# One attention-and-SwiGLU kernel on one core: the opening by sets, the short last set as one quarter, and DMAs in other slots of the schedule

## The chip, the core and the metric

The kernel runs on one core of a Trainium2 chip. The core has TensorE (PE, matmuls and weight loads), VectorE (DVE), ScalarE (ACT), GpSimd (POOL) and SyncE (SP), which here only issues DMAs. Each engine executes its own instructions in order and waits on semaphores for the others. The metric is device time in microseconds (us) of one execution, the median of several.

## The reference

Four batches (B) of N = 12416 tokens with C = 128 channels go through an induced set attention with m = 32 inducing points, and the result through a normalized SwiGLU feed-forward of 1536 hidden channels. Cut to what matters:

```python
def mab(q, kv):
    s = scale * (q @ kv.transpose(0, 2, 1))
    s = s - s.max(-1, keepdims=True)
    a = np.exp(s)
    a /= a.sum(-1, keepdims=True) + 1e-09
    return a @ kv
h = mab(I, x)                 # 32 rows per batch
attn = mab(x, h)              # 12416 rows per batch
# then, for every token:
rms = np.sqrt(np.mean(x * x, axis=-1, keepdims=True) + 1e-06)
xn = x / rms * rms_g
g = xn @ w_gate
silu = g * (1.0 / (1.0 + np.exp(-g)))
val = xn @ w_val
out = silu * val @ w_out
```

The three weight matrices arrive as 64-bit floats and have to be rounded to 32 bits on the chip; `x` and the inducing points are 32-bit.

## The kernel before

**Tiling.** The 97 blocks of 128 tokens of a batch are cut into seven sets: five of 16 blocks, one of 15 and a short last one of 2 (`per`). A set is four quarters of 32 partitions each. The attended row of a token is a combination of the 32 rows of `h`, so the normalized input of the feed-forward is 32 weights per token (`a`, scaled by `rs`) times `h`; the gate and value matrices are therefore folded with `h` into two stacks of 32 rows per batch (`sg`, `sv`). Both the weights and the stacks are split in a high and a low half (`hi`, `lo`), and four combinations of halves, 4 x 32 = 128 rows, make one matmul. A **unit** is one quarter of a set, up to 512 tokens; the short set is one unit of 256 tokens, for which its four quarters are put side by side. So a batch has 25 units.

**The feed-forward** (`ffn`) runs one unit in 12 **steps**, one for each 128 hidden channels: a gate matmul (L460), a value matmul (L462), silu on ACT (L464), a product `u` on DVE (L466), and two steps later the output matmul into `acc` (L448; 32-bit, in two passes). After the last step DVE transposes `acc` into `o` (L451) and four DMAs store it (L455); for the short set sixteen do.

**What a unit needs.** `gather` (L434) brings the quarter's `hi` and `lo` rows four times under each other into a moving tile `a`: four DMAs on SP, sixteen for the short set. It is issued at step 2 of the unit before. `hi` and `lo` come from the steps of `seam`: `turn_a`, `square`, `scale`, `apply` and `split`. `split` transposes the weights (L419), casts them into `hi` (L421) and writes the rest into `lo` (L422). The pool `halves` has one buffer, so `split` of a set waits until the gather of the last unit of the set before has landed. In the table `seams`, `split` stands at step 4 of the third unit of the set before.

**Two batches at once.** While the 300 steps of a batch run, `schedule` puts the attention of the next batch between them, each piece at a step number `k` from 0 to 299: transposes of x, `scores1`, the maxima, one exponential over the whole batch (`exp1`), `turn_e` and `sum_h` by set, `end_h`, `turn_h`, `square_h`, the fetches of the gate and value weights (`fetch`, L352), `stack`, and the second scores and softmax. `sum_h` also issues the loads of the rows of x of the batch after the next one (`load_rows`, L115), as soon as the set's tile is used. `stack` multiplies the weights with `h` (L361), rounds and splits them, and issues the 12 DMAs that place them in the stack (L371). All these DMAs go through SP in the order in which the code issues them; at most eight are under way.

**The opening.** The first batch has no feed-forward to hide behind. Its x is loaded by rows, transposed on PE (L248) and copied by ACT (L251); `scores1`, the maxima, `exp1` and `sum_h` follow. Between these pieces `convert` puts the rounding of nine weight chunks of 128 x 512: six DVE passes and three POOL passes for each (L204 to L216), cut into six steps. A chunk's buffer is free for the next raw chunk when its result has been stored (L188). Then follow `stack` for both matrices, the first set's `seam`, the first gather, and unit 0.

The order on every engine is thus written by hand: by the order of the calls in the opening, and by the step numbers of `schedule` and `seams` after it.

Of the kernel before, what the change touches and what calls it, by code (L numbers as in the profile page):

```python
# [18 lines left out]
P = 128  # L19
R = 4  # L20
# [4 lines left out]
def kernel(  # L25
# [32 lines left out]

    nc = tc.nc
# [10 lines left out]
    assert N % P == 0 and full >= 2 and rest < 12  # L70
    per = [16] * full if not rest else [16] * (full - 1) + [15, rest + 1]
    NS = len(per)
    start = [P * sum(per[:s]) for s in range(NS)]
    cols = [slice(m * sum(per[:s]), m * sum(per[:s + 1])) for s in range(NS)]
    SCW = N // R

    units = [(s, q, 1) for s in range(full) for q in range(R)] + [(s, 0, R) for s in range(full, NS)]
    assert all(per[s] * nq <= 16 for s, _, nq in units)
# [23 lines left out]
    def of(dram, b, s):  # L102

        d = dram[ds(b * N + start[s], P * per[s]), :]
        return d.rearrange("(i q t) c -> q i t c" if b else "(q i t) c -> q i t c", q=R, i=m)
# [4 lines left out]
    def load_rows(b, s):  # L110
        n = per[s]
        t = xnat[b, s] = xnp.tile([P, n, C], F32, name=f"xn{s}")
        if b:
# [63 lines left out]
    def load_w(i, c):  # L177
# [14 lines left out]
        if not wide:  # L192
# [4 lines left out]
        e, s = (up.tile([P, 512], I32, name="u") for _ in range(2))  # L197
        f = astk.tile([P, 512], F32, name="a")
        r = outp.tile([P, 512], F32, name="o")
        fi = f.bitcast(I32)  # L200
        ve = nc.vector
        ge = ve if (i, c) == (1, NC - 1) else nc.gpsimd
        return [
            lambda: ve.tensor_scalar(out=e[:], in0=high, scalar1=20, scalar2=0x7FF,  # L204
                                     op0=ALU.logical_shift_right, op1=ALU.bitwise_and),
            lambda: ve.tensor_scalar(out=e[:], in0=e[:], scalar1=896.0, scalar2=1151.0, op0=ALU.max, op1=ALU.min),
            lambda: ve.tensor_scalar(out=s[:], in0=high, scalar1=-(1 << 31), scalar2=0x3F800000,
                                     op0=ALU.bitwise_and, op1=ALU.bitwise_or),
            lambda: (ve.tensor_scalar(out=fi[:], in0=high, scalar1=12, scalar2=9,
                                      op0=ALU.logical_shift_left, op1=ALU.logical_shift_right),  # L210
                     ge.tensor_scalar(out=e[:], in0=e[:], scalar1=-896.0, scalar2=float(1 << 23), op0=ALU.add, op1=ALU.mult)),
            lambda: ve.scalar_tensor_tensor(out=r[:], in0=low.bitcast(U32), scalar=2.0 ** -52, in1=s.bitcast(F32)[:],
                                            op0=ALU.mult, op1=ALU.mult),
            lambda: (ve.tensor_tensor(out=fi[:], in0=fi[:], in1=s[:], op=ALU.bitwise_or),
                     ge.tensor_tensor(out=f[:], in0=f[:], in1=r[:], op=ALU.add),
                     ge.tensor_tensor(out=dst, in0=f[:], in1=e.bitcast(F32)[:], op=ALU.mult),  # L216
                     put()),
        ]
# [3 lines left out]
    def attention(b, load_next):  # L222
# [12 lines left out]
        def turn_x(s, k):  # L235
# [9 lines left out]
            if now:  # L245
# [5 lines left out]
                nc.scalar.copy(out=dst, in_=src)  # L251

        def scores(s, lhsT):
            w = per[s] * m
            ps = bank()
            for q in range(R):
                nc.tensor.matmul(ps[ts(q, m), 0:w], lhsT, xT[b, s][:, ts(q, w)], start=True, stop=True)  # L257
            return ps[:, 0:w]

        def scores1(s):  # L260
            nc.vector.tensor_scalar(out=sc[b][:, cols[s]], in0=scores(s, indT[:]), scalar1=1.0, scalar2=None,
# [21 lines left out]
        def exp1():  # L283
            hl = st["hl"] = once.tile([P, C + 1], F32, name="hl")
            nc.scalar.activation(sc[b][:], sc[b][:], AF.Exp, bias=st["nbias"][:], scale=SCALE, accum_out=hl[:, C:C + 1])  # L285

        def turn_e(s):
            e = st["e", s] = work.tile([P, per[s] * m], F32, name="e", tag="work")
            nc.vector.transpose(out=e[:], in_=sc[b][:, cols[s]])

        def sum_h(s):
# [3 lines left out]
            ps = bank()  # L295
# [7 lines left out]
            if load_next:  # L303
                load_rows(b + 1, s)
# [337 lines left out]
```

## Time and profile before

| what | value |
|---|---|
| median of 3 runs | 1890.85 us (1885.89 to 1890.9) |
| the profiled execution's own time | 1892.92 us |
| its span (first to last instruction) | 1891.1 us |
| mean granted PE clock | 0.962 of full speed |
| PE busy | 1731.8 us, 92% |
| DVE, ACT, POOL busy | 1141.6, 757.4, 176.8 us |
| first matmul of the feed-forward | at 94.1 us |
| last matmul | ends at 1881.2 us |

A row of a wait view reads: the engine and line that waited, what it waited for, the total, how often, and the longest. A row of a timeline reads: start, duration, engine, line, operation, output and inputs, count; in brackets the engine's idle time before it and what ended that. SPq is SP's queue of DMA issues: the time there is that of issuing, not that of the transfer. PE's matmul rows overlap; the distance from start to start tells the pace.

### The profile page before, as it was taken

How to read it: one execution, taken by the hardware profiler on the slowest of the kernel's cores; microseconds unless marked ns; L12 is line 12 of the kernel's file. 1: busy time of each engine (PE TensorE's matmuls, PEld its weight loads, DVE VectorE, ACT ScalarE, POOL GpSimd, SP SyncE). 2: the span in 40 equal slices, each digit the busy share in tenths (PEclk: the TensorE clock that was granted, in tenths of full speed). 3: DMA queues.
4: the chain of work that ended last, by engine and by line, in shares of the span. 5: the costliest groups of instructions: out<-in, count | busy, mean ns of one | idle time of the engine just before them, and what ended most of it. 6: DMA issues, size and time to landing. Idle time of an engine off the chain costs nothing.

```text
span 1891.1 us, 20393 instructions
## 1 busy us (share of the span) xinstructions
PE 1731.8 (92%) x6258; PEld 961.9 (51%) x6258; DVE 1141.6 (60%) x1998; ACT 757.4 (40%) x1256; POOL 176.8 (9%) x141
## 2 busy tenths in 40 slices
PE   6199999989979999998997999998998999999997
PEld 4045555545545555554555555554454655555554
DVE  5567765546546776565654776564655665655654
ACT  3044444323524444532453444532353444444443
POOL 2221110101011011010110110110101101100100
PEclk8599999989989999999998999998998999999998
DMA  7744313533324212434333311122111211111111
GB/s 271 173 77 84 58 32 70 127 76 57 58 45 78 45 25 40 94 95 92 59 57 61 66 37 29 27 48 57 42 33 19 40 30 28 34 34 33 28 36 19
DMA packets 393517, 114.05 MB, mean 60 GB/s; under 512 B 369056, under 2 KB 373184, under 8 KB 390848
## 3 DMA queue, kind: packets, MB, share of 16 engines
q1 hardware_dynamic: 393216, 112.73, 29.0%
q8 instruction: 50, 0.82, 0.2%
q14 instruction: 59, 0.48, 0.1%
q10 hardware_dynamic: 192, 0.02, 0.0%
HBM read 53.95 MB, written 27.00 MB: 43 GB/s over the span
## 4 chain that ended last, share of the span: by engine, by line
PE 82%; DMA 5%; SPq 5%; DVE 3%; ACT 2%; issue 2%; POOL 0%; DVEq 0%; ACTq 0%
PE acc L448 50%; PE gv L460 14%; PE gv L462 13%; SPq L434 3%; DMA xn<-in_x_dram 2%; DMA a<-lo 2%; PE mm L257 2%; DVE u L466 1%; PE mm L398 1%; DMA a<-hi 1%; PE mm L297 1%; ACT silu L464 1%; SPq L455 1%; PE gv L257 0%; ACT sc L285 0%
## 5 line engine op out<-in xcount | busy, mean ns | idle before, releaser
L448 PE MATMUL acc<-u,wo 128*128 128x512 f32 (+2 forms) x2400 | 1220.9, 592 | 58.5 <-DVE u L466 58.2
L466 DVE TENSOR_TENSOR u<-silu,gv 128x512 f32<-128x512 f32 (+2 forms) x1200 | 796.4, 670 | 606.6 <-ACT silu L464 594.0
L464 ACT ACTIVATE silu<-gv 128x512 f32<-128x512 f32 (+2 forms) x1200 | 699.4, 584 | 1046.4 <-PE gv L460 545.3
L460 PE MATMUL gv<-a,sg 128*128 128x512 f32 (+2 forms) x1200 | 932.2, 777 | 60.1 <-DMA a<-lo 57.1
L448 PEld LDWEIGHTS acc<-u,wo 128*128 128x128 f32 x2400 | 444.9, 191 | 216.1 <-DVE u L466 73.4
L462 PE MATMUL gv<-a,sv 128*128 128x512 f32 (+2 forms) x1200 | 471.3, 393 | 0.6 <-DVE u L466 0.6
L460 PEld LDWEIGHTS gv<-a,sg 128*128 128x128 f32 x1200 | 230.9, 192 | 348.9 <-issue 326.3
L462 PEld LDWEIGHTS gv<-a,sv 128*128 128x128 f32 x1200 | 231.1, 193 | 276.4 <-issue 193.0
L401 POOL TENSOR_TENSOR z<-z,sc 128x512 f32<-128x512 f32 (+2 forms) x27 | 30.3, 1124 | 1125.6 <-DVE z L400 1104.8
L409 POOL TENSOR_TENSOR rs<-ms,mhalf 128x16 f32<-128x16 f32 (+2 forms) x28 | 71.9, 2568 | 107.2 <-DVE ms L407 107.2
L451 DVE STREAM_TRANSPOSE o<-acc 128x512 f32<-128x512 f32 (+2 forms) x100 | 69.1, 691 | 3.7 <-PE acc L448 3.4
L341 POOL TENSOR_TENSOR sc<-sc,mx 128x512 f32<-128x512 f32 (+2 forms) x24 | 21.9, 914 | 354.5 <-DVE mx L340 354.5
L421 DVE CAST hi<-aT 128x512 fp32r<-128x512 f32 (+2 forms) x28 | 11.0, 391 | 70.0 <-DMA a<-hi 64.7
L240 DVE STREAM_TRANSPOSE xT<-xT 128x512 f32<-128x512 f32 (+2 forms) x84 | 53.1, 633 | 0.0
L398 PE MATMUL mm<-eT,gram 128*128 128x512 f32 (+2 forms) x56 | 27.2, 568 | 5.6 <-DVE eT L389 5.6
L414 POOL TENSOR_TENSOR sc<-sc,rs 128x512 f32<-128x512 f32 (+2 forms) x27 | 25.1, 928 | 2.1
L422 DVE TENSOR_TENSOR lo<-aT,hi 128x512 fp32r<-128x512 f32 (+2 forms) x28 | 17.4, 621 | 11.2 <-DMA a<-lo 10.7
L464 ACT ACT_TABLE_LOAD x8 | 10.3, 1283 | 26.7 <-PE gv L460 26.6
L297 PE MATMUL mm<-xn,e 128*32 128x128 f32 x582 | 20.7, 276 | 0.0
L400 DVE STREAM_TRANSPOSE z<-mm 128x512 f32<-128x512 f32 (+2 forms) x28 | 17.9, 639 | 3.5 <-PE mm L398 3.5
L257 PE MATMUL mm<-xT,indT 128*32 128x512 f32 (+2 forms) x168 | 20.0, 547 | 0.0
L257 PE MATMUL mm<-xT,hT 128*32 128x512 f32 (+2 forms) x168 | 20.0, 547 | 0.0
(126 smaller groups left out, 421.8 us busy)
## 6 DMA issues: line engine op xcount, KB each, us to landing
out_dram<-o SPq DMA_DIRECT2D x320, 64.0 KB, 2.0
xn<-in_x_dram SPq DMA_DIRECT2D x60, 256.0 KB, 4.9
xT<-in_x_dram SPq DMA_DIRECT2D x60, 256.0 KB, 4.6
a<-hi SPq DMA_DIRECT2D x160, 64.0 KB, 2.0
a<-lo SPq DMA_DIRECT2D x160, 64.0 KB, 2.0
w<-w SPq DMA_DIRECT2D x21, 256.0 KB, 3.1
xn<-in_x_dram SPq DMA_DIRECT2D x5, 1024.0 KB, 11.4
out_dram<-o SPq DMA_DIRECT2D x64, 60.0 KB, 2.0
```

What stands on the lines that cost most here:

```text
L240: nc.vector.transpose(out=t[:, ts(k, n * m)], in_=t[:, ts(k, n * m)])
L257: nc.tensor.matmul(ps[ts(q, m), 0:w], lhsT, xT[b, s][:, ts(q, w)], start=True, stop=True)
L297: nc.tensor.matmul(ps[ts(t % R, m), 0:C], e[:, ts(t, m)], xn[:, t, :], start=t < R, stop=t + R >= n)
L398: nc.tensor.matmul(ps[:, 0:n * m], gram[b][:], st["eT"][:], start=True, stop=True)
L409: nc.gpsimd.tensor_tensor(out=rs[:, 0:n], in0=ms[:, 0:n], in1=mhalf[:, 0:n], op=ALU.pow)
L434: nc.sync.dma_start(out=a[ts(k, m), ts(q, w)].bitcast(F32), in_=half[ts(q0 + q, m), 0:w].bitcast(F32))
L448: nc.tensor.matmul(acc[:, 0:T], wo[:, j, :], t[:, 0:T], start=(j == 0), stop=(j == NJ - 1))
L451: nc.vector.transpose(out=o[:, 0:T], in_=acc[:, 0:T])
L460: nc.tensor.matmul(g[:, 0:T], sg[:, ts(j, P)], a[:, 0:T], start=True, stop=True)
L462: nc.tensor.matmul(v[:, 0:T], sv[:, ts(j, P)], a[:, 0:T], start=True, stop=True)
L464: nc.scalar.activation(sl[:, 0:T], g[:, 0:T], AF.Silu)
L466: nc.vector.tensor_tensor(out=t[:, 0:T], in0=sl[:, 0:T], in1=v[:, 0:T], op=ALU.mult)
```

## The change

**The short set as one quarter.** For the second half of the attention and the feed-forward, the short set is now 32 partitions by 8 blocks instead of 128 by 2 (`quarters`, `per2`, `rows2`, `cols2`). Its softmax, `seam` and exponential work on 32 partitions, its exponential is an instruction of its own (`exp2`), and its unit takes four gathering and four storing DMAs.

**The opening.** One exponential for each set (`exp1_of`) and one PSUM bank for the sums of all sets. A chunk's rounding is now four DVE passes, two POOL passes and two ACT passes, in two parts (`parts`, `join`). Every fourth block of transposed x is copied by DVE instead of ACT. The stacks of the first batch are written by `stack_of`: `hg` holds 128 columns, four copies of 32, so that one matmul for each chunk gives all four row groups; ACT casts all of them and DVE subtracts in the lower half. No DMA places them. The first gather issues its `lo` halves from ACT's queue.

**Slots.** `load_rows` of the next batch moves from `sum_h` (and for batch 1 from the opening) to steps 97, 103, ... of the schedule. The second `fetch` moves from step 178 to 193, the second `stack` from 198 to 203, and the placing DMAs go one row group per step (`place`). `split` moves from step 4 to step 9. A store is issued two steps after its transpose (`soon`).

```diff
-    units = [(s, q, 1) for s in range(full) for q in range(R)] + [(s, 0, R) for s in range(full, NS)]
+    quarters = [R] * full + [1]
+    per2 = per[:full] + [R * per[full]]
+    rows2 = [slice(0, m * nq) for nq in quarters]
+    cols2 = columns(per2)
...
+        def parts():
+            ve.tensor_scalar(out=e[:], in0=high, scalar1=20, scalar2=0x7FF, op0=ALU.logical_shift_right, op1=ALU.bitwise_and)
+            nc.gpsimd.tensor_scalar(out=e[:], in0=e[:], scalar1=896.0, scalar2=1151.0, op0=ALU.max, op1=ALU.min)
+            nc.scalar.activation(e[:], e[:], AF.Copy, bias=-896.0 * (1 << 23), scale=float(1 << 23))
+            ve.tensor_scalar(out=f[:], in0=high, scalar1=0xFFFFF, scalar2=None, op0=ALU.bitwise_and)
+            nc.scalar.activation(f.bitcast(F32)[:], f[:], AF.Copy, bias=1.0, scale=2.0 ** -20)
+
+        def join():
+            ve.scalar_tensor_tensor(out=e[:], in0=high, scalar=-(1 << 31), in1=e[:], op0=ALU.bitwise_and, op1=ALU.bitwise_or)
+            ve.scalar_tensor_tensor(out=f.bitcast(F32)[:], in0=low.bitcast(U32), scalar=2.0 ** -52, in1=f.bitcast(F32)[:],
+                                    op0=ALU.mult, op1=ALU.add)
+            nc.gpsimd.tensor_tensor(out=dst, in0=f.bitcast(F32)[:], in1=e.bitcast(F32)[:], op=ALU.mult)
+            put()
...
-                nc.scalar.copy(out=dst, in_=src)
+                if k == 1:
+                    nc.vector.tensor_copy(out=dst, in_=src)
+                else:
+                    nc.scalar.copy(out=dst, in_=src)
...
+        def exp1_of(s):
+            if not s:
+                st["hl"] = once.tile([P, C + 1], F32, name="hl")
+                st["ls"] = small.tile([P, NS], F32, name="gmx")
+            part = sc[b][:, cols1[s]]
+            nc.scalar.activation(part, part, AF.Exp, bias=st["nbias"][:], scale=SCALE, accum_out=st["ls"][:, s:s + 1])
+            if s + 1 == NS:
+                nc.vector.reduce_sum(out=st["hl"][:, C:C + 1], in_=st["ls"][:], axis=AX.X)
...
-            if load_next:
-                load_rows(b + 1, s)
...
-            for k, half in enumerate((hi, hi, lo, lo)):
-                for c in range(NC):
-                    nc.sync.dma_start(out=stacks[b][i][ts(k, m), ts(c, 512)].bitcast(F32),
-                                      in_=half[ts(c, m), :].bitcast(F32))
+        def place(i, k):
+            half = st["halves", i][k // 2]
+            for c in range(NC):
+                nc.sync.dma_start(out=stacks[b][i][ts(k, m), ts(c, 512)].bitcast(F32), in_=half[ts(c, m), :].bitcast(F32))
+
+        def stack_of(i, c):
+            ps = bank()
+            nc.tensor.matmul(ps[:], st["hg"][:], w0.pop((i, c))[:], start=True, stop=True)
+            w, low = stacks[b][i], slice(P // 2, P)
+            nc.scalar.copy(out=w[:, ts(c, 512)], in_=ps[:])
+            nc.vector.tensor_tensor(out=w[low, ts(c, 512)], in0=ps[low, :], in1=w[low, ts(c, 512)].bitcast(F32),
+                                    op=ALU.subtract)
...
         for k, half in enumerate((hi, lo, hi, lo)):
-            for q in range(nq):
-                nc.sync.dma_start(out=a[ts(k, m), ts(q, w)].bitcast(F32), in_=half[ts(q0 + q, m), 0:w].bitcast(F32))
+            queue = nc.scalar if (b, u) == (0, 0) and k % 2 else nc.sync
+            queue.dma_start(out=a[ts(k, m), 0:w].bitcast(F32), in_=half[ts(q, m), 0:w].bitcast(F32))
...
+                soon(2, lambda: store(o))
...
-    for k in ("max1", "max2", "max3", "exp1"):
+    for k in ("max1", "max2", "max3"):
         f[k]()
-    convert(6)
-    for s in range(NS + 1):
-        if s < NS:
-            f["turn_e"](s)
-        if s:
-            f["sum_h"](s - 1)
+    for s in range(NS):
+        f["exp1_of"](s)
+        if not s:
+            convert()
+        f["turn_e"](s)
+        f["sum_h"](s)
+    convert()
...
+                add(97 + 6 * s, load_rows, b + 1, s)
...
-                add(170 + 8 * i, g["fetch"], i)
-                add(191 + 7 * i, g["stack"], i)
+                add(175 + 18 * i, g["fetch"], i)
+                add(191 + 12 * i, g["stack"], i)
+                for k in range(R):
+                    add(193 + 12 * i + k, g["place"], i, k)
...
-                n, j = ((1, 2), (1, 6), (1, 9), (1, 9), (2, 4))[i] if k else ((2, 1), (2, 4), (2, 7), (2, 7), (3, 0))[i]
+                n, j = ((1, 2), (1, 6), (1, 9), (1, 9), (2, 9))[i] if k else ((2, 1), (2, 4), (2, 7), (2, 7), (3, 0))[i]
```

How the instructions stand on the engines, at three places. First ACT in the opening, from the copies of set 1 on, before up to the one exponential. `xT_...` are the transposed x of a set, `u` and `a` a chunk's exponent and mantissa. Before:

```order
L251 COPY xT_191<-gv 128x4x4x32 x4
L251 COPY xT_230<-gv 128x4x4x32 x4
L251 COPY xT_269<-gv 128x4x4x32 x4
L251 COPY xT_308<-gv 128x4x4x32 x4
L251 COPY xT_347<-gv 128x4x4x32 x3
L251 COPY xT_347<-gv 128x3x4x32
L251 COPY xT_385<-gv 128x2x4x32
L285 ACTIVATE sc,hl<-sc,nbias 128x3104
```

And now:

```order
L259 COPY xT_194<-gv 128x4x4x32 x3
L212 ACTIVATE u<-u 128x512
L214 ACTIVATE a<-a 128x512
L259 COPY xT_233<-gv 128x4x4x32 x3
L212 ACTIVATE u<-u 128x512
L214 ACTIVATE a<-a 128x512
L259 COPY xT_272<-gv 128x4x4x32 x3
L259 COPY xT_308<-gv 128x4x4x32 x3
L212 ACTIVATE u<-u 128x512
L214 ACTIVATE a<-a 128x512
L259 COPY xT_347<-gv 128x4x4x32 x2
```

The copies of three of the sets now have two passes of a chunk ahead of them (a fourth chunk's passes stand behind the last copy).

Second, SP at the end of the opening, up to the first gather. `w_119` and `w_120` are stores of rounded chunks. Before:

```order
L115 DMA xn_586<-in_x_dram 32x1920 x4
L115 DMA xn_595<-in_x_dram 32x256 x4
L188 DMA w_119<-silu 128x512
L371 DMA sg<-whi 32x512 x6
L371 DMA sg<-wlo 32x512 x6
L188 DMA w_120<-silu 128x512
L371 DMA sv<-whi 32x512 x6
L371 DMA sv<-wlo 32x512 x6
L434 DMA a<-hi 32x512
```

And now:

```order
L180 DMA sg<-in_moe_w_out_dram 128x4x256
L196 DMA w_119<-silu 128x512
L196 DMA w_120<-silu 128x512
L462 DMA a<-hi 32x512 x2
L132 DMA xT_686<-in_x_dram 32x64x32 x4
```

The 28 row loads of batch 1 (the last two of seven rows are shown) and the 24 placing DMAs have left this stretch.

Third, SP at the end of the first batch, from the last 480-token gather to the first gather of batch 1. Before:

```order
L455 DMA out_dram<-o 480x1x32 x4
L434 DMA a<-hi 32x64 x4
L434 DMA a<-lo 32x64 x4
L434 DMA a<-hi 32x64 x4
L434 DMA a<-lo 32x64 x4
L124 DMA xT_4025<-in_x_dram 32x64x32
L124 DMA xT_4312<-in_x_dram 32x64x32
L455 DMA out_dram<-o 480x1x32 x4
L434 DMA a<-hi 32x512
```

And now:

```order
L462 DMA a<-hi 32x256
L462 DMA a<-lo 32x256
L462 DMA a<-hi 32x256
L462 DMA a<-lo 32x256
L492 DMA out_dram<-o 480x1x32 x4
L132 DMA xT_3942<-in_x_dram 32x64x32
L132 DMA xT_4217<-in_x_dram 32x64x32
L462 DMA a<-hi 32x512
```

The short unit's gather has four DMAs instead of sixteen, and a store stands behind the gather of its unit instead of ahead of it.

231 lines of the change are left out of this document (115 added, 116 removed).

## The prediction

> **What bounds the kernel now.** I read the page first, then the engines' busy time by stretches, then the waits of TensorE (PE), VectorE (DVE) and the DMA queue (SP), and last the chain of waits and the timelines at the places that these named. From the page and from the view by stretches (span; PE, weight loads, DVE, ACT and POOL busy; granted clock, DMA share, GB/s):
>
> ```profile
> span 1891.1 us, 20393 instructions
> PE 1731.8 (92%) x6258; PEld 961.9 (51%) x6258; DVE 1141.6 (60%) x1998; ACT 757.4 (40%) x1256; POOL 176.8 (9%) x141
> ...
> 100.00:1891.00 1791.00, 1687.88 (x5866) 935.51 (x5865) 1085.74 (x1873) 735.50 (x1222) 149.06 (x110) 0.98 0.27 51
> 0.00:100.00 100.00, 43.88 (x393) 26.42 (x394) 55.90 (x126) 21.87 (x35) 27.70 (x31) 0.72 0.76 218
> ```
>
> After 100 us PE is busy nearly all the time and nothing else is near its limit, so PE is the bound, and what can be won is its idle time (103 us there), its half-rate time, and the opening (56 us idle). Who ends PE's waits from 96 us on, who ends DVE's, and who ends SP's (total us, times, longest):
>
> ```profile
> PE acc L448 <- DVE u L466: 58.2, 22, 9.5
> PE gv L460 <- DMA a<-lo: 30.7, 7, 9.0
> ```
>
> ```profile
> DVE hi L421 <- DMA a<-hi: 64.7, 22, 7.8
> DVE lo L422 <- DMA a<-lo: 10.7, 19, 2.1
> ```
>
> ```profile
> SPq L455 <- DVE o L451: 827.4, 83, 15.9
> SPq L352 <- PE mm L361: 80.4, 3, 29.4
> ```
>
> PE waits 58.2 us for products `u` and 30.7 us for moving tiles `a`. The products are late because DVE itself sits in `split`: its cast into `hi` must not overwrite the single buffer while the gather of the set's last unit still reads it (64.7 us). And the gather is late because SP, one queue in order, stands behind stores whose `o` isn't transposed (827 us, mostly free, but not when a gather is next) and behind weight fetches whose buffers PE frees only later (80.4 us in 3). One such wait in the chain (start, us):
>
> ```profile
> 354.30 0.72 DVE o L451
> ...
> 355.04 0.61 SPq L455
> ...
> 357.70 1.15 SPq L352
> ...
> 360.43 0.59 SPq L434
> ...
> 361.06 2.52 DMA a<-hi
> ...
> 363.71 0.44 DVE hi L421
> ```
>
> Four stores and three fetches go before the gather, and DVE's cast waits for its landing. PE's timeline at that place, and at the longest wait for `a`:
>
> ```profile
> 365.51 2.07 PE L448 MATMUL acc<-u,wo 128*128 128x512 f32 x2 [3.13 <-DVE u L466]
> ...
> 368.24 1.28 PE L448 MATMUL acc<-u,wo 128*128 128x512 f32 x2
> ...
> 369.81 1.02 PE L448 MATMUL acc<-u,wo 128*128 128x512 f32 x2
> ...
> 371.13 1.02 PE L448 MATMUL acc<-u,wo 128*128 128x512 f32 x2
> ```
>
> ```profile
> 400.62 0.77 PE L460 MATMUL gv<-a,sg 128*128 128x512 f32 x1 [9.00 <-DMA a<-lo]
> ...
> 401.62 1.91 PE L448 MATMUL acc<-u,wo 128*128 128x512 f32 x2
> ...
> 404.18 1.91 PE L448 MATMUL acc<-u,wo 128*128 128x512 f32 x2
> ```
>
> A step of the feed-forward takes 371.13 - 369.81 = 1.32 us. After the wait of 3.13 us the next two take 2.73 and 1.57: 1.7 us more. After 9.00 us the two that follow take 2.56 and 2.45, and the start 0.5 more: 2.9 us. So a long wait is paid twice, as idle time and as slow matmuls behind it.
>
> **The change part by part.** The sum is made against the profiled execution, whose own time is 1892.92 for a span of 1891.1; the median shown is 1890.85, so I take span and median as one.
>
> *Split, store and gather: -58.2 us.* `split` moves from step 4 to step 9 of the set's third unit. The gather of the last unit still goes out at step 2, so 7 steps (9.2 us) lie between instead of 2 (2.6 us). The gather takes four issues of 0.63 (below) and a landing of 2.0 to 2.5 us, 5 us in all. The store now goes out two steps after its transpose, which puts it behind the gather. At a batch boundary the price was largest:
>
> ```profile
> 536.22 2.47 SPq L434 DMA_DIRECT2D a<-hi  x4
> ...
> 543.80 2.49 SPq L434 DMA_DIRECT2D a<-lo  x4
> ```
>
> ```profile
> 545.04 0.43 DVE L421 CAST hi<-aT 128x512 fp32r<-128x512 f32 x1 [7.81 <-DMA a<-hi]
> 547.51 0.69 DVE L422 TENSOR_TENSOR lo<-aT,hi 128x512 fp32r<-128x512 f32 x1 [2.04 <-DMA a<-lo]
> ```
>
> Sixteen issues for the short set's unit fill 10 us; as one quarter it needs four. What is late next: the gather of the next set's first unit follows `split` after 5 steps instead of 10, but has 10 steps (13 us) until it is read. I find no wait that keeps its cause, and take all 58.2; the bound below is half of it, if SP stays as late as now.
>
> *Waits for `a`: -30.7 us.* Three are at unit 16 of batches 0 to 2: the second fetch stood on SP from step 178, waiting for matmuls of step 191, with unit 16's gather (issued at 182) behind it. It is now issued at 193, and the 24 placing DMAs go three to a step instead of twelve at once. Then SP carries 3 fetches, 12 placings, 4 gathers and 4 stores in unit 16, 23 issues of about 0.6 = 14 us against 15.8 us: it fits, with 2 us to spare, so I add 1 us for the products that wait for a `work` buffer there. The other four waits are at the short unit, whose twelve fewer gathers and twelve fewer stores take 15 us of issue off SP per batch.
>
> *Half-rate matmuls: -27 us.* From below, six long waits (three at unit 16, three at batch boundaries) times 2.9 = 17; from above, the missing 2% of the clock over 1791 us = 36. I take the middle, since the dozen shorter waits cost up to 1.7 each. [...] The row at 365.51, slow after 3.13 us, says that shorter waits cost too, so I stay with 27.
>
> *The opening: -10 us.* It has gains and a loss. The rows, by engine (SP, PE, ACT, POOL):
>
> ```profile
> 45.79 26.64 SPq L115 DMA_DIRECT2D xn<-in_x_dram  x23
> ...
> 73.98 3.77 SPq L371 DMA_DIRECT2D sg<-whi  x6
> ...
> 92.03 0.58 SPq L434 DMA_DIRECT2D a<-lo  x1
> ```
>
> ```profile
> 38.33 4.14 PE L297 MATMUL gv<-xn,e 128*32 128x128 f32 x96 [4.42 <-DVE e L289]
> ...
> 94.12 0.77 PE L460 MATMUL gv<-a,sg 128*128 128x512 f32 x1 [26.36 <-DMA a<-lo]
> ```
>
> ```profile
> 15.73 2.05 ACT L251 COPY xT<-gv 128x512 f32<-128x512 f32 x4 [1.00 <-PE gv L248]
> ...
> 34.13 2.88 ACT L285 ACTIVATE sc<-sc,nbias 128x3104 f32<-128x3104 f32 x1 [6.55 <-DVE nbias L281]
> ...
> 96.25 1.09 ACT L464 ACTIVATE silu<-gv 128x512 f32<-128x512 f32 x2
> ```
>
> ```profile
> 16.76 0.72 POOL L211 TENSOR_SCALAR u<-u 128x512 int32<-128x512 int32 x1 [15.39 <-DVE u L206]
> 20.39 1.28 POOL L215 TENSOR_TENSOR a<-a,o 128x512 f32<-128x512 f32 x1 [2.91 <-DVE a L214]
> ...
> 62.53 3.04 POOL L409 TENSOR_TENSOR rs<-ms,mhalf 128x16 f32<-128x16 f32 x1 [3.79 <-DVE ms L407]
> ```
>
> (a) Until the exponentials, +6.5. A converted chunk loses two DVE passes and a POOL product, and gains two ACT passes, which the trace doesn't show; I price them as ACT's copies of that size, 0.51 to 0.59. ACT takes them in order, before the next set's copies. The first waits for POOL's clamp, which ends at 17.5; two passes end at 18.7, while the copies of set 2 now start at 15.73: 3 us late. Sets 3 and 5 have the same wait (2 us each), and PE, whose banks these copies free, passes it on. DVE's shorter part gives back half a microsecond. Below: 0, if the wait hides; above: 13.
> (b) The sums, -1. Set 0's exponential is a sixth of 2.88 and a read, 0.8; with a join and a transpose PE starts 2.1 us after the bias instead of 4.2, and loses 1 to its cold clock.
> (c) From `h` to the power, -1: the same operations in another order.
> (d) From the power to the first unit, -16. Now it ends at 65.6 and PE starts at 94.12, 28.5 later: SP is in the next batch's row loads until 72.4, and then issues 24 placings. Both are gone, since TensorE writes all four copies of the stack itself. In their place, after the power: three POOL operations (1.28 + 0.72 + 1.28), a matmul, a cast and a subtraction (2.2), apply and split (2.5), half of the gather on SP and half on ACT (two issues, 1.2, and landing, 2.0), and hand-overs: 12.7.
> (e) +1.3: the last chunks' ACT passes stand ahead of the first silu and wait for POOL. The gathers of units 1 and 2 also wait for POOL's last products, with row loads and stores behind them on SP; these products end some 4 us after PE's start, and unit 1 comes 16 us after it, so that costs nothing.
> So PE starts at about 83. Both ends of (a) give -16.5 to -3.5.
>
> *The end: -5.5 us.* SP's and DVE's last rows:
>
> ```profile
> 1873.58 15.51 SPq L455 DMA_DIRECT2D out_dram<-o  x20
> ```
>
> ```profile
> 1881.26 0.45 DVE L451 STREAM_TRANSPOSE o<-acc 128x256 f32<-128x256 f32 x1 [0.79 <-PE acc L448]
> ```
>
> From 1881.7 sixteen stores take 7.4 us; four take 1.9.
>
> *Small: +2 us.* The second exponential becomes two instructions, about 0.4 more in each batch beside PE's 1.32 per step, and the 1 us at unit 16. Moved row loads (28 DMAs in units 8 to 11) fall on a queue that is otherwise free there.
>
> Sum: 1891.1 - 58.2 - 30.7 - 27 - 10 - 5.5 + 2 = 1762.
>
> **The rivals.**
> *The opening gives nothing.* If ACT's wait behind POOL costs twice as much and the conversions hold the last stack back, PE starts at 94 as now: 1772 to 1775. For it: the POOL row stands on the way twice. Against: 28.5 us of SP work are truly gone.
> *Waits come back.* Loads of 256 KB pass at 26.64 / 23 = 1.16 us each, so four of them ahead of a gather cost 4.6 us, and eight 9.3; with its 5 us that is more than the 13 us it has. If this happens in two units of each of the three batches, and unit 16 keeps a few microseconds, some 20 of the 89 us stay and 10 of the clock: 1792. At its worst (four units each, 4 us): 1830.
> *Slower: the clock gives way under unbroken load.* The waits may be what lets PE run at full rate between them. PE's work at full rate is 1688 - 27 = 1661, all else 101; the time is 1661/c + 101, and with a mean clock c below 0.928 it is over 1891 (0.90 gives 1947). Against it: the clock is 0.98 with PE 94% busy, and the low stretches stand behind waits. [...]
> *It doesn't do what it says* would need the sixteen gathers or the early row loads to be there still; the instruction order shows neither.
>
> **How the numbers follow.** Forecast 0.65 (1762, own range 1748 to 1778); opening without gain 0.14; waits come back 0.16 (1792, tail to 1830); clock 0.03; something that eats all of it unseen 0.02. The range takes the clock's and the opening's lower ends together (1762 - 9 - 6.5 = 1746) and reaches to the waits that return: 1743 to 1796. About 0.3% is what a measurement of this kernel tells from no change; all cases but the last two are faster by far more. Faster 0.94, same 0.02, slower 0.04.
>
> **What would show it.** Right: PE's waits on `u` and `a` after the opening fall from 89 to under 10 us; the cast into `hi` waits for no gather; the granted clock from 100 us on is 1.00 to two digits; PE's first gate matmul stands at 80 to 87 us and the bias is ready near 40 instead of 34; the last store is issued within 3 us of the last transpose. Wrong: waits for `a` in units 9 to 12 or 17 and 18, a start after 90, or a clock under 0.96 without waits before it.

## The result, and the profile after

The changed kernel takes **1761.6 us** (median of 4 runs, 1759.28 to 1761.64) against 1890.88 for the kernel before on the same chip: a ratio of 0.9317, with a 95% interval of 0.9298 to 0.9336. That is 129.3 us less; the forecast was 1762, in a range of 1743 to 1796. The profiled execution took 1761.64 us for a span of 1759.6. From its page and from the view by stretches (columns as in the prediction):

```profile
span 1759.6 us, 20237 instructions
PE 1707.2 (97%) x6234; PEld 955.4 (54%) x6234; DVE 1144.2 (65%) x1982; ACT 769.0 (44%) x1288; POOL 188.4 (11%) x135
...
0.00:100.00 100.00, 58.05 (x419) 34.60 (x420) 54.40 (x119) 34.99 (x67) 34.90 (x28) 0.78 0.48 151
100.00:1755.00 1655.00, 1649.11 (x5817) 920.80 (x5815) 1089.79 (x1864) 734.04 (x1221) 153.51 (x107) 1.00 0.30 59
```

From 100 us to its last matmul PE idles for some 5 us instead of 93 (the prediction's 103 hold 10 us behind the last matmul), and the granted clock is 1.00 instead of 0.98. What is left of PE's waits from 80 us to the end (total, times, longest):

```profile
PE gv L496 <- DMA a<-lo: 8.1, 1, 8.1
PE gv L265 <- ACT silu L500: 3.4, 1, 3.4
PE gv L496 <- ACT silu L500: 2.4, 3, 0.8
PE gv L498 <- ACT silu L500: 1.3, 6, 0.2
PE gv L498 <- DVE u L502: 0.6, 3, 0.2
```

The row of 58.2 us for `u` at the output matmul is gone. The row for `a` has one entry, and that one is the first gather of the opening. DVE's waits show no row of `hi` or `lo` waiting for a gather. The opening, by engine (POOL, ACT, PE):

```profile
17.12 2.02 POOL L211 TENSOR_SCALAR u<-u 128x512 int32<-128x512 int32 x1 [15.75 <-DVE u L210]
...
65.92 3.24 POOL L439 TENSOR_TENSOR rs<-ms,mhalf 128x16 f32<-128x16 f32 x1 [7.16 <-DVE ms L437]
```

```profile
38.01 0.63 ACT L212 ACTIVATE u<-u 128x512 int32<-128x512 int32 x1 [4.03 <-POOL u L211]
...
39.06 0.71 ACT L301 ACTIVATE sc<-sc,nbias 128x512 f32<-128x512 f32 x1
...
85.36 0.63 ACT L212 ACTIVATE u<-u 128x512 int32<-128x512 int32 x1 [2.48 <-POOL u L211]
...
87.82 1.09 ACT L500 ACTIVATE silu<-gv 128x512 f32<-128x512 f32 x2
```

```profile
40.75 8.21 PE L319 MATMUL gv<-xn,e 128*32 128x128 f32 x194 [2.55 <-DVE e L307]
...
70.44 2.07 PE L394 MATMUL gv<-silu,hg 128*128 128x512 f32 x2 [6.31 <-POOL silu L220]
...
83.05 0.77 PE L496 MATMUL gv<-a,sg 128*128 128x512 f32 x1 [8.13 <-DMA a<-lo]
```

The first gate matmul stands at 83.05 instead of 94.12 (11.1 us earlier), the first silu at 87.82 instead of 96.25 (8.4 us earlier). At the other end the last transpose starts at 1754.19 and the last eight stores are issued by 1757.24; from the end of that transpose to the end of the span there are 5.0 us instead of 9.4.

```profile
1754.19 0.45 DVE L483 STREAM_TRANSPOSE o<-acc 128x256 f32<-128x256 f32 x1 [0.79 <-PE acc L480]
```

```profile
1747.09 10.15 SPq L492 DMA_DIRECT2D out_dram<-o  x8
```

### The profile page after: what moved, and what is told of

It is laid out like the page before. It is cut to its first block, busy times and chain, and to the rows that moved or that the text cites. A ratio compares the mean times of both kernels' runs of the same rounds, so it can differ in the third digit from the quotient of the medians.

```text
span 1759.6 us, 20237 instructions
## 1 busy us (share of the span) xinstructions
PE 1707.2 (97%) x6234; PEld 955.4 (54%) x6234; DVE 1144.2 (65%) x1982; ACT 769.0 (44%) x1288; POOL 188.4 (11%) x135
## 3 DMA queue, kind: packets, MB, share of 16 engines
q1 hardware_dynamic: 388944, 111.02, 30.7%
## 4 chain that ended last, share of the span: by engine, by line
PE 92%; ACT 3%; DVE 2%; POOL 1%; issue 1%; DMA 1%; SPq 0%; DVEq 0%; ACTq 0%; POOLq 0%
PE acc L480 55%; PE gv L496 15%; PE gv L498 15%; PE mm L265 2%; PE mm L428 1%; PE mm L319 1%; ACT silu L500 1%; POOL u L211 1%; PE gv L265 1%; DMA xn<-in_x_dram 1%; ACT L500 1%; ACT sc L294 0%; PE gv L319 0%; ACT sc L367 0%; PE mm L380 0%
## 5 line engine op out<-in xcount | busy, mean ns | idle before, releaser
L480 PE MATMUL acc<-u,wo 128*128 128x512 f32 (+2 forms) x2400 | 1200.1, 583 | 0.3
L496 PE MATMUL gv<-a,sg 128*128 128x512 f32 (+2 forms) x1200 | 922.4, 769 | 10.9 <-DMA a<-lo 8.1
L480 PEld LDWEIGHTS acc<-u,wo 128*128 128x128 f32 x2400 | 440.4, 188 | 151.0 <-issue 58.5
L498 PE MATMUL gv<-a,sv 128*128 128x512 f32 (+2 forms) x1200 | 465.8, 388 | 1.9 <-ACT silu L500 1.3
L439 POOL TENSOR_TENSOR rs<-ms,mhalf 128x16 f32<-128x16 f32 (+2 forms) x28 | 75.9, 2711 | 116.6 <-DVE ms L437 116.6
L212 ACT ACTIVATE u<-u 128x512 int32<-128x512 int32 x9 | 5.7, 630 | 39.3 <-POOL u L211 39.3
L211 POOL TENSOR_SCALAR u<-u 128x512 int32<-128x512 int32 x9 | 18.2, 2018 | 35.3 <-DVE u L210 35.1
L253 PE MATMUL gv<-ident,xn 128*128 128x128 f32 x97 | 15.6, 326 | 5.9 <-ACT xT L259 3.5
```

Of the source, the lines that this page charges most:

```text
L211: nc.gpsimd.tensor_scalar(out=e[:], in0=e[:], scalar1=896.0, scalar2=1151.0, op0=ALU.max, op1=ALU.min)
L439: nc.gpsimd.tensor_tensor(out=rs, in0=ms, in1=mhalf[rows, 0:n], op=ALU.pow)
L480: nc.tensor.matmul(acc[:, 0:T], wo[:, j, :], t[:, 0:T], start=(j == 0), stop=(j == NJ - 1))
L496: nc.tensor.matmul(g[:, 0:T], sg[:, ts(j, P)], a[:, 0:T], start=True, stop=True)
L498: nc.tensor.matmul(v[:, 0:T], sv[:, ts(j, P)], a[:, 0:T], start=True, stop=True)
```

## The experiments

The number was right; what the runs had to find out is whether its terms were. The kernel before was timed again with every set of runs and its median lay between 1890.86 and 1894.58 us, so two kernels of different sets are told apart only from some 4 us on. Where a difference is near that, the trace decides. Unless it says otherwise, an experiment is the changed kernel with one thing undone.

| kernel | median us | ratio to before (95%) | against changed |
|---|---|---|---|
| changed | 1761.6 | 0.9317 (0.9298 to 0.9336) | |
| A: split back at step 4 | 1758.56 | 0.9301 (0.9287 to 0.9315) | -3.0 |
| B: store at once | 1762.79 | 0.9324 (0.9310 to 0.9338) | +1.2 |
| A and B | 1797.25 | 0.9507 (0.9491 to 0.9523) | +35.7 |
| C: sixteen pieces | 1764.73 | 0.9332 (0.9308 to 0.9355) | +3.1 |
| A, B and C | 1837.82 | 0.9713 (0.9687 to 0.9739) | +76.2 |
| D: old slots of fetch and placing | 1784.88 | 0.9439 (0.9422 to 0.9455) | +23.3 |
| A, B, C and D | 1875.83 | 0.9922 (0.9905 to 0.9938) | +114.2 |
| row loads early | 1774.63 | 0.9385 (0.9362 to 0.9409) | +13.0 |
| first stacks placed by DMA | 1762.73 | 0.9321 (0.9298 to 0.9344) | +1.1 |
| clamp on DVE | 1757.54 | 0.9291 (0.9268 to 0.9315) | -4.1 |
| clamp on DVE, joins first | 1747.36 | 0.9239 (0.9225 to 0.9253) | -14.2 |
| before, with split at step 9 alone | 1829.69 | 0.9670 (0.9652 to 0.9688) | +68.1 |

### A, B and both: which slot cures the late products

```diff
-  ((1, 2), (1, 6), (1, 9), (1, 9), (2, 9))[i] if k
+  ((1, 2), (1, 6), (1, 9), (1, 9), (2, 4))[i] if k        # A
```

> The changed kernel with split back at step 4 of the set's third unit; nothing else undone. The set's last gather goes out at step 2 and needs 2.5 us of issuing and 2.0 to 2.5 of landing, so the cast into hi, 2.6 us after it, should wait 2 to 2.6 us in each of some 22 sets. Theory (the later step carries most of the 58.2 us): DVE waits 45 to 57 us for the gathers, PE waits 20 to 40 us for products u, some 10 more are lost at half rate: 1790 to 1810 us. Rival (issuing the gather ahead of the store is enough, and DVE at 65% takes a wait of 2 us without PE noticing): PE waits under 10 us for u, 1760 to 1768 us.

```diff
-                soon(2, lambda: store(o))
+                store(o)                                    # B
```

> The changed kernel with the four stores issued right behind the transpose, ahead of the next gather, as before; split stays at step 9. Theory (7 steps, 9.2 us, are more than the 2.5 us of four more issues and the 5 us of the gather): the cast waits at no or few places, 1760 to 1767 us. Rival (the store waiting on SP for a late transpose is what made the gather late, so the order on SP is needed too): DVE waits for gathers in ten or more sets, PE waits 15 us or more for u, 1775 to 1795 us.

> Both of these undone together: split at step 4 and stores at once; the short set stays one quarter, fetches and placings stay in their new slots. Theory (these two slots are the whole of the 58.2 us except what the sixteen gathers of the short unit cost): 40 to 60 us of waits for u and 10 to 15 at half rate: 1810 to 1830 us. Rival (the short unit's sixteen pieces caused the most): under 1785 us.

A measured 1758.56 and B 1762.79: neither costs anything, and the theory for A, 1790 to 1810, is wrong. Together they cost 35.7 us, less than the 48 to 68 of the theory and more than the 23 at most of the rival. So each of the two slots is enough by itself. The reason is in SP's and DVE's timelines at the same set boundary. With A alone:

```profile
743.66 0.51 SPq L462 DMA_DIRECT2D a<-hi  x1
...
745.70 0.58 SPq L462 DMA_DIRECT2D a<-lo  x1
...
761.02 1.96 SPq L492 DMA_DIRECT2D out_dram<-o  x4
```

```profile
760.28 0.71 DVE L483 STREAM_TRANSPOSE o<-acc 128x512 f32<-128x512 f32 x1
...
764.98 0.43 DVE L449 CAST hi<-aT 128x512 fp32r<-128x512 f32 x1
```

The set's last gather is issued from 743.66 to 746.28, 18.7 us before the cast that must wait for it, and ahead of the transpose and the store of 760 us. With A and B:

```profile
776.91 1.95 SPq L492 DMA_DIRECT2D out_dram<-o  x4
778.96 0.51 SPq L462 DMA_DIRECT2D a<-hi  x1
...
780.78 0.59 SPq L462 DMA_DIRECT2D a<-lo  x1
```

```profile
776.17 0.71 DVE L483 STREAM_TRANSPOSE o<-acc 128x512 f32<-128x512 f32 x1
...
782.31 0.43 DVE L449 CAST hi<-aT 128x512 fp32r<-128x512 f32 x1 [1.47 <-DMA a<-hi]
```

Now the gather stands behind the store, the store behind its transpose, and the cast comes 3.4 us after the gather's first issue. A step number is a place in the order of a queue and no time: SP runs ahead of PE by as much as the next instruction that has to wait lets it. Putting the store two places later lets the gather run ahead by most of a unit.

### C, and A, B and C: the sixteen pieces

```diff
-            queue.dma_start(out=a[ts(k, m), 0:w], in_=half[ts(q, m), 0:w])
+            pieces = R if s == full else 1
+            for z in range(pieces):
+                queue.dma_start(out=a[ts(k, m), ts(z, w // pieces)], in_=half[ts(q, m), ts(z, w // pieces)])
... the stores likewise, in pieces of two blocks
```

> The changed kernel, in which only the short unit's four gathers are cut into sixteen, each of a quarter of the columns, and its four stores into sixteen: the same bytes, twelve more issues of about 0.6 us twice per batch. Theory (the issues alone cost SP's time): at the end sixteen stores take 7.4 us instead of 1.9 (+5.5), and at each batch boundary the gather is landed only 12 us after its start, so PE waits 0 to 3 us for a and the cast of the next set 2 to 5 us: 1768 to 1785 us. Rival (all but the end is hidden): 1764 to 1768 us, no cast waits for a gather.

> The changed kernel with split at step 4, stores at once, and the short unit's gathers and stores in sixteen pieces; fetches and placings stay in their new slots. Alone, the first two together cost 35.7 us and the third 3.1. Theory (the pieces make the gather at the three batch boundaries 7.5 us later, which only the early cast meets: three waits of 9 us for u instead of 1 to 2.6, each with 2 to 3 us at half rate behind it): 1824 to 1836 us. Rival (the pieces cost their end alone, and the old fetches make the rest of what all of them together cost): 1798 to 1805 us.

C alone costs 3.1 us and no wait for `u` or `a` comes back: the rival of the first expectation, all but the end hidden. A, B and C together cost 76.2 us, 37 more than 35.7 + 3.1: the theory of the second. By its ratio to the kernel before in the same set the time is 1836.6 us on the scale of the others, just above what was expected. SP and DVE at the first batch boundary of that kernel:

```profile
510.38 2.59 SPq L464 DMA_DIRECT2D a<-hi  x4
...
518.07 2.49 SPq L464 DMA_DIRECT2D a<-lo  x4
```

```profile
519.35 0.43 DVE L449 CAST hi<-aT 128x512 fp32r<-128x512 f32 x1 [7.94 <-DMA a<-hi]
```

PE's waits there are 9.78, 8.91 and 9.04 us for `u`, one at each of the three boundaries. By groups its waits after the opening are these, with A and B first, then with A, B and C:

```profile
PE acc L480 <- DVE u L502: 27.5, 21, 2.6
```

```profile
PE acc L482 <- DVE u L508: 49.9, 22, 9.8
```

### D, and all four

```diff
-                add(175 + 18 * i, g["fetch"], i)
-                add(191 + 12 * i, g["stack"], i)
+                add(170 + 8 * i, g["fetch"], i)
+                add(191 + 7 * i, g["stack"], i)
                 for k in range(R):
-                    add(193 + 12 * i + k, g["place"], i, k)
+                    add(191 + 7 * i, g["place"], i, k)
```

> The changed kernel with the second batch's weight fetch, stack and placings in their old slots (fetches at steps 170 and 178, stacks at 191 and 198, each with its twelve placings at once), in batches 0 to 2. Theory: unit 16's gather stands on SP behind a fetch that waits for matmuls of step 191, three waits of 8 to 9 us for a and 2.9 us at half rate behind each: 1789 to 1797 us. Rival (the gather's delay is hidden now that the stores have left its place on SP): under 10 us of waits for a, 1760 to 1768 us.

> The changed kernel with all of this undone at once: split at step 4, stores at once, fetches, stacks and placings in their old slots, the short unit's gathers and stores in sixteen pieces; the new opening and the new row load slots stay. Theory (the causes add up, as they cost alone: 35.7 + 23.3 + 3.1 us over 1761.6): 1818 to 1830 us. Rival (they are one cause, SP's lateness, that grows when they meet; the parts of my sum, 58 + 31 + 27 + 5.5, less nothing): 1865 to 1885 us, with waits for u and a of 75 to 90 us and a clock of 0.98.

D alone costs 23.3 us, under the 27 to 35 expected. The mechanism is the theory's, with shorter waits. SP's wait in front of the fetch and PE's for the gather behind it:

```profile
SPq L373 <- PE mm L380: 85.2, 3, 28.6
```

```profile
PE gv L496 <- DMA a<-lo: 16.2, 3, 5.5
```

With A, B and C undone as well the same three waits are 7.04, 6.93 and 6.96 us. All four undone cost 114.2 us. The parts alone, 35.7 + 23.3 + 3.1, make 62.1; so 52 us are interaction: 37 arise where the sixteen pieces meet the early cast (A, B and C), and the other 15 where the old fetches join them. The rival's numbers hold: 1875.83 us, with 58.0 us of waits for `u` and 25.4 for `a` after the opening, against 58.2 and 30.7 in the kernel before. In all these places a gather is late on SP; that this is one cause, and not two that lie on one queue, is the reading of these sums.

### One edit on the kernel before

```diff
-  ((1, 2), (1, 6), (1, 9), (1, 9), (2, 4))[i] if k        # in the kernel before
+  ((1, 2), (1, 6), (1, 9), (1, 9), (2, 9))[i] if k
```

> The kernel before with one edit alone: split at step 9 instead of 4. Theory (either the later split or the later store keeps the cast clear of the gather by itself, as each did alone in the changed kernel): PE's waits for u fall from 58.2 to 5 to 15 us, DVE's for gathers from 75 to under 20, the waits for a stay near 31: 1825 to 1845 us. Rival (here SP is later, with twelve more gathers and twelve more stores at each short unit and the early row loads, so the later step alone doesn't reach): half of the 58.2 us stay, 1855 to 1870 us.

It takes 1829.69 us, 62 less than before. Its waits of PE from 100 us on:

```profile
PE gv L460 <- DMA a<-lo: 37.1, 10, 9.0
...
PE acc L448 <- DVE u L466: 2.2, 3, 1.0
```

One pair of numbers gives almost half of the whole gain. The theory holds, and more than it asked for `u`: the 58.2 us become 2.2, at the boundaries too. The waits for `a` were to stay near 31 and rose to 37.1; they need the other edits.

### The opening: placings, row loads, clamp

```diff
-    for i in range(2):
-        f["stack_of"](i, 0)
     scale()
     convert(3)
-    for c in range(1, NC):
-        for i in range(2):
-            f["stack_of"](i, c)
+    for i in range(2):
+        f["st"]["w", i] = [w0.pop((i, c)) for c in range(NC)]
+        f["stack"](i)
+        for k in range(R):
+            f["place"](i, k)
```

> The changed kernel with the first batch's stacks made as in the other batches: three matmuls per matrix into 32 rows each, cast and difference on DVE, and 24 placing DMAs on SP, instead of three matmuls that write all four copies; row loads stay in their new slots. Theory (24 issues of 0.6 us are 14 to 15 us on the way to the first unit, less 2 to 3 us for fewer casts): PE's first gate matmul at 93 to 97 us instead of 83, 1771 to 1776 us. Rival (SP was only late because of the row loads, so the placings overlap with the seam of set 0): start by 87 us, 1761 to 1766 us.

The first gate matmul is at 87.86 us, 4.8 later than in the changed kernel and far from the 93 to 97 of the theory; the time is 1762.73. So the rival holds, if for a start 0.9 us later than its 87: with the row loads out of the way the placings overlap with the seam of set 0. They take SP's queue from 69.85 to 85.02; ACT issues its half of the first gather at 80.92, when the seam is done, and only the 4.2 us from there to SP's half at 85.12 are the placings' own.

```diff
             elif end:
                 nc.vector.tensor_copy(out=hl[:, 0:C], in_=ps[:, 0:C])
+            if load_next:
+                load_rows(b + 1, s)
...
-                add(97 + 6 * s, load_rows, b + 1, s)
```

> The changed kernel with the row loads of the next batch back behind each set's sums: 28 in the opening, 28 in units 12 to 15 of batches 0 and 1. Theory (no placings stand behind them any more, and the queue is otherwise free in those units): the first gather at 78.6 us is past them, 1760 to 1766 us. Rival (the stores and raw reads of the last weight chunks stand behind them, and gathers of units 13 to 16 do too): start after 87 us or waits for a of 5 us and more, 1770 to 1780 us.

The time is 13.0 us longer, as in the rival, but not for its reason. SP's, ACT's and PE's rows:

```profile
58.49 2.62 SPq L123 DMA_DIRECT2D xn<-in_x_dram  x3
...
83.29 0.86 SPq L123 DMA_DIRECT2D xn<-in_x_dram  x2
```

```profile
81.18 1.24 ACTq L464 DMA_DIRECT2D a<-lo  x2
```

```profile
98.48 0.76 PE L498 MATMUL gv<-a,sg 128*128 128x512 f32 x1 [21.66 <-DMA a<-hi]
```

Sixteen of the 28 loads are out by 61.1 us. Then SP stands until 83.29, and the view of waits says for what:

```profile
SPq L123 <- DMA a<-lo: 22.4, 2, 22.1
```

A row load waits for the `lo` halves of the first gather, which ACT issues. The program keeps at most eight DMAs under way (eight at once is the most in the traces of the kernel before and of the changed one) and gives them eight semaphores in turn, SP's and ACT's together. In its order, with the semaphore that each waits for, the first of the fifth set's loads takes a place behind ACT's `lo`:

```
31 L123 DMA xn_494<-in_x_dram 32x2048 [waits DMAHW0_49]
32 L123 DMA xn_494<-in_x_dram 32x2048 [waits DMAHW3_49]
...
38 L123 DMA xn_542<-in_x_dram 32x2048 [waits DMAHW1_49,PE_49]
```

Semaphores 1 and 2 are left out once: ACT's two DMAs have them. So this run doesn't price the row loads. It shows a wait that the early loads make with another part of the same change, the `lo` halves on ACT's queue; in the kernel before the 28 loads took SP only from 42.44 to 72.44. The theory's reason, that 28 loads would be done before the gather at 78.6, is neither shown nor refuted: twelve loads take 7.2 us once they may go (83.29 to 90.46), and sixteen were out at 61.1. Later than the opening no wait for `a` comes back; there the same loads are hidden.

```diff
-            nc.gpsimd.tensor_scalar(out=e[:], in0=e[:], scalar1=896.0, scalar2=1151.0, op0=ALU.max, op1=ALU.min)
+            ve.tensor_scalar(out=e[:], in0=e[:], scalar1=896.0, scalar2=1151.0, op0=ALU.max, op1=ALU.min)
```

> The changed kernel with the clamp of the exponents on DVE instead of POOL, where it takes 2.02 us each; DVE's passes of the same size and type take 0.42. Theory (ACT's conversion passes, in order ahead of the copies of transposed x and of the stacks' casts, wait for this clamp): ACT's waits of 3.6 to 4.0 us before these passes fall by about 1.5, the bias is ready at 35.5 to 37 us instead of 38.2, PE's first gate matmul stands 2 to 4 us earlier: 1756 to 1759.5 us. Rival (DVE is itself on the way, and a pass more on it costs what POOL gives back): start within 1 us of 83, 1760 to 1762 us.

As the theory has it: 1757.54 us, and the first gate matmul at 80.86. The clamp's group in the changed kernel, with who waited for it, and in this one (duration in ns, shortest, median, longest):

```profile
L211 POOL TENSOR_SCALAR u<-u x9: 1921/2021/2147, 17.1 to 83.2; 128x512 int32<-128x512 int32 x9
...
  ACT u L212: 39.3, 9
```

```profile
L211 DVE TENSOR_SCALAR u<-u x9: 426/427/1371, 16.9 to 79.8; 128x512 int32<-128x512 int32 x9
...
  ACT u L212: 19.3, 8
```

### A version that beats both

```diff
     turn_a()
+    tails.pop(0)()
     square()
-    for i in range(2):
-        f["stack_of"](i, 0)
+    tails.pop(0)()
     scale()
-    convert(3)
-    for c in range(1, NC):
+    for c in range(NC):
         for i in range(2):
             f["stack_of"](i, c)
...
-            for k in range(2):
+            for k in range(3):
                 add(k, convert)
```

> The changed kernel with the clamp on DVE, and with the last two gate and value chunks joined before the mean square and the power of set 0 instead of after, so that POOL multiplies them out ahead of its 3.2 us power; then all six stack matmuls in a row, apply, split and gather; the last chunk's passes go to step 0. Theory (PE's wait of 6.4 us for POOL's product, and DVE's of 3.1 us for the casts behind it, are on the way to the first gather): the first gate matmul at 71 to 75 us instead of 80.9, 1748 to 1752 us. Rival (the power, now after two more products and two joins, ends so much later that apply is no earlier; or the chunks of the output matrix come too late for the first output matmuls): start after 79 or a wait for wo, 1755 to 1759 us.

`tails` holds the second halves (`join`) of chunks whose first halves have been issued. The kernel takes 1747.36 us, ratio 0.9239 (0.9225 to 0.9253), 14 us under the changed kernel and 10 under the one with the clamp on DVE alone; that is 0.6 us below the theory's range, with the first gate matmul inside its own. POOL's and PE's rows:

```profile
60.66 1.27 POOL L220 TENSOR_TENSOR silu<-a,u 128x512 f32<-128x512 f32 x1 [1.83 <-DVE a L218]
62.32 2.92 POOL L439 TENSOR_TENSOR rs<-ms,mhalf 128x16 f32<-128x16 f32 x1 [0.39 <-DVE ms L437]
```

```profile
62.95 1.12 PE L394 MATMUL gv<-w,hg 128*128 128x512 f32 x2 [1.31 <-DVE sg L397]
...
72.89 0.77 PE L496 MATMUL gv<-a,sg 128*128 128x512 f32 x1 [7.96 <-DMA a<-lo]
```

The products now end before the power starts, PE's wait of 6.31 us for a product behind the power is gone, and the first gate matmul is 10.2 us earlier than in the changed kernel. What remains on the way is the power itself and 8 us for the first gather.

## Why the prediction was right, point by point

**The bound** was PE's idle and half-rate time after 100 us, and that is where most of the time came from. Undoing the four slot and piece edits brings back 114.2 of the 129.3 us.

**Split, store and gather, -58.2.** The total was right: 58.2 us became nothing. The working was right in one half: 7 steps between gather and cast instead of 2 are enough, since in the kernel before the later step alone leaves 2.2 us. It was wrong in the other: "the gather of the last unit still goes out at step 2". With the later store the gather goes out as soon as nothing before it on SP waits, most of a unit ahead of its step. So the change holds two cures for one wait, and the sum counted them as one term without seeing that either would do; that the same working made undoing the step cost 28 to 48 us, and it cost nothing, is this error. The rows of 16 gathers at the boundary were read rightly, but got no price of their own: over the three boundaries it is 37 us, and only where the cast is early.

**Waits for `a`, -30.7.** Right in size, and in place for the three long ones at unit 16: the old fetch slots alone bring back 16.2 us in three waits. The other four, 7 us in the kernel before, were put down to the sixteen pieces; these alone bring back none, but 4.8 us in four waits come back when A, B and C are undone together. The sum's guess that unit 16 keeps 1 us was not seen.

**Half-rate matmuls, -27.** Counting the time by which PE's steps exceed their usual pace, in places that lose over 1 us each, the kernel before has 32.7 us in sixteen places and the changed one 3.2 in three; these three, of 1.1 us each, are in both, so 29.4 us in thirteen places are gone. The granted clock itself falls to one half in thirteen stretches there, which cost 26 us of PE's time. The middle between 17 and 36 was a fair choice and no more: it was not worked out which waits cost the clock, and the reason given was only half right, below.

**The opening, -10.** The gate matmul came 11.1 us earlier, the first silu 8.4. By its parts: (a) the exponentials start 4.9 us later (39.06 against 34.13), 6.5 expected, though POOL's clamp took 2.02 us and not the 0.72 that the sum took from a row of another operation; part of ACT's wait was hidden. (b) From the exponential to the end of the sums 2.0 us were gained instead of 1; the cold clock that the sum counted is in the traces, 0.50 from 40.75 to 44.85 us in the changed kernel and 0.67 from 38.33 to 42.50 in the kernel before. (c) From there to the power 0.5 was lost instead of 1 gained, since two of the first stacks' differences stand ahead of the mean square on DVE. (d) From the power's end to the gate matmul 13.9 us instead of 28.5, -14.7 for -16. In (d) "SP is in the next batch's row loads until 72.4, and then issues 24 placings" gives the two one price. Without the loads, the placings cost the first gate matmul 4.8 us and the time 1.1; what the loads alone cost stays open. (e) was mis-sized: the first silu stands 4.8 us behind the gate matmul instead of 2.1, +2.6 for +1.3, because two clamps of 2 us, not 0.72, stand in front of it. That also explains why placing the first stacks by DMA costs the gate matmul 4.8 us and the time only 1.1: there the silu at 89.46 is 1.6 us behind it, waiting for the same ACT passes.

**The end, -5.5.** 4.4 in the traces, 3.1 in the time when the stores are cut again.

**Small, +2.** The feed-forward's waits for silu and `u` at its gate and value matmuls are 4.3 us in the rows above, of 2.4, 1.3 and 0.6, and were 3.3 before: +1.0.

With these sizes the sum is 1891.1 - 58.2 - 30.7 - 29.4 - 8.4 - 4.4 + 1.0 = 1761.0, against 1759.6 measured. That the forecast of 1762 came nearer than its terms is luck in part: the half-rate time was 2.4 us larger than its term, the opening's and the end's gains 1.6 and 1.1 smaller, and these cancel.

**The rivals.** "The slower clock under unbroken load" is refuted by the row from 100 us on: PE 99.6% busy at 1.00. "Waits come back" and "the opening gives nothing" did not happen in the changed kernel; the early row loads show how near the latter was, with the gate matmul at 98.48. **The signs** named for right were seen: waits under 10 us after the opening, no gather in front of `hi`, the start at 83. The bias was ready at 38.24, between the 34 before and the 40 expected, and the last store was issued 2.6 us after the last transpose.

What stays open is what the opening's edits are worth one by one: the row loads could not be priced without the wait that they made, and the exponentials by set, ACT's share in the conversion and DVE's copies were not undone by themselves.

## What to carry to other kernels

A DMA's slot in a hand-written order is a place in its queue: ask what stands ahead of it and waits (for data, a buffer or a semaphore that another queue's transfer holds), not at which step it is written. Two edits against one wait can each be enough, and undone together with a third they can cost twice their sum, so price a chain by what meets in it and not item by item. And take a duration from a row of the same operation, not only of the same engine, shape and type.

## What the runs showed of the hardware

**POOL's price depends on the operation.** On 128 x 512 int32 its add and multiply took 0.72 us in the kernel before (median of eight), its max and min 2.02 us in the changed one (nine); on DVE max and min took 0.43. The two groups on the same engine, the kernel before's:

```profile
L211 POOL TENSOR_SCALAR u<-u x8: 718/722/787, 16.8 to 98.5; 128x512 int32<-128x512 int32 x8
```

**Which waits cost the clock.** In the traces of the kernel before and of the changed one PE's granted clock is 1.00 or 0.50, and it changes only on a grid of steps of 3.41 us. In the kernel before it falls thirteen times from 100 us to the last matmul, for one, two or three steps. Two of that kernel's waits, and the steps around them (behind each stretch stand its length and PE's busy time; the granted clock is the column after POOL):

```profile
286.44 1.73 PE L448 MATMUL acc<-u,wo 128*128 128x512 f32 x2 [1.88 <-DVE u L466]
...
585.02 0.48 PE L460 MATMUL gv<-a,sg 128*128 128x512 f32 x1 [2.85 <-DMA a<-lo]
```

```profile
283.41:286.82 3.41, 1.53 (x5) 0.67 (x4) 2.15 (x4) 0.83 (x2) 0.00 (x0) 1.00 0.24 58
286.82:290.23 3.41, 3.41 (x8) 1.66 (x6) 1.76 (x6) 0.60 (x1) 0.00 (x0) 0.50 0.24 58
...
580.37:583.78 3.41, 1.80 (x6) 0.63 (x4) 1.38 (x2) 0.61 (x2) 0.00 (x0) 1.00 0.28 62
583.78:587.19 3.41, 2.17 (x7) 1.43 (x8) 0.69 (x1) 0.94 (x2) 0.00 (x0) 1.00 0.67 113
587.19:590.61 3.42, 3.42 (x12) 1.89 (x10) 3.13 (x5) 1.45 (x3) 0.00 (x0) 1.00 0.59 94
```

The wait of 1.88 us lies within one step, and the step behind it runs at half rate. The longer one, of 2.85 us, is shared by two steps with 1.61 and 1.24 us of idle time, and costs nothing. In the kernel before, from 100 us to its last matmul, there are thirteen full-rate steps with a half-rate step behind them, and PE idled for 1.88 us or more in each of them. Twenty others had 0.8 us or more of idle time and full rate behind them: 1.61 us at most. The changed kernel has one such step, with 0.83 us, and no fall. So in these two traces the idle time within one step tells the cases apart, somewhere between 1.61 and 1.88 us of its 3.41, and for a wait between 1.9 and about 3.8 us (twice 1.88, an estimate) its place on the grid decides: in the kernel before waits of 2.57 and 2.69 us were followed by a fall, those of 2.62 and 2.85 us were not. A step at half rate costs 3.41 / 2 = 1.7 us, an estimate from its length; the two steps of the feed-forward behind the wait of 3.13 us lost as much (2.73 and 1.57 us instead of 1.32 each), and it is the size that the prediction gave to "the dozen shorter waits". Of the waits of 0.9 to 3.2 us in the kernel before, seven cost such a step and thirteen nothing.
